# Queries and keys loaded in long runs, tokens in another order, in an attention and feed-forward kernel

## The chip, the cores and the metric

The kernel runs on one core of one Trainium2 chip. The metric is the device time of one execution in microseconds. TensorE is called PE below, VectorE DVE, ScalarE ACT, GpSimd POOL, and SyncE, which here only issues transfers, SP.

## What is computed

Attention with normalised queries and keys, for 8 batches, 12 heads, 448 tokens and 64 columns, and then a feed-forward block on the 3584 tokens (768 columns in, 1024 inside). All is float32; the feed-forward weights arrive as float64.

```python
q_n, k_n = rmsnorm(q, g_q), rmsnorm(k, g_k)          # over the 64 columns
scores = q_n @ k_n.T / sqrt(64)
attn = exp(scores - max); attn = attn / (sum(attn) + 1e-9)
x = (attn @ v) as (3584, 768)                        # heads side by side
h = x @ w_in                                         # (3584, 1024)
solu = h * softmax(h)
ln = (solu - mean) / sqrt(var + 1e-6) * g_ln
out = ln @ w_out                                     # (3584, 768)
```

The result doesn't depend on the order in which the keys are summed, and each token's row stands by itself from the attention to the output. So tokens may be held in any order inside, as long as the output rows are written to their places.

## The kernel before

The work has three stages that follow each other on PE: attention (to about 326 us), the first product of the feed-forward block (L982, to about 579 us) and the second (L1177, to the end). The two products are done in blocks that are added and subtracted first, so that seven products stand for eight; this has no part in the change.

**Attention.** Two heads of a batch make a pair (48 of them, `n`), and two pairs make a quad (24, `m`; its pairs are `a = 2m` and `b = 2m + 1`). A loop runs over the quads. The instructions of each engine are issued in the order in which the loop writes them, and each engine keeps its order. `unit(f)` runs a piece of PE work and then whatever was put off by `later`.

For each pair, except the first two, the loop calls these functions:

- `load(n)` (L627 to L637) reads q and k of the pair with eight transfers on SP's queue. A transfer takes 32 partitions. Partition `g * 32 + t` holds, for each of 14 blocks of 32 tokens, token `t` of that block: half a row, 32 columns (128 bytes). `g` stands for the head and the half of the columns. The tile `qk` has five buffers.
- `squares(n)` (L653) squares the tile on ACT, `row_sums(n)` (L660) sums each 32 columns on DVE, and `fold_sums(m)` (L668) adds the two halves of a row for a whole quad on POOL: four copies between partitions and a sum. `fold_one(n)` (L677) does it on DVE for one pair.
- `rsqrt_seed` (L690) makes the inverse root on ACT by Ln and Exp, and `rsqrt_step` (L697) improves it on DVE by a Newton step of four instructions.
- `normalise(n)` (L706) multiplies the tile by it on POOL, one instruction of 128 x 896.
- `qk_transpose(n)` (L720) transposes blocks of 32 x 32 on DVE, which gives `qkT` with the columns on the partitions and the tokens along them, and `gain(n)` (L725) multiplies the q half by the gains on ACT.
- `scores(n, kc)` (L804) makes three tiles of 128 keys, `scores_last(m)` (L818) the last 64 keys of both pairs. ACT takes the exponentials (L802). `values_last` and `values` (L846, L859) multiply by v, and `sums(m)` (L870) makes the row sums on PE from the last tile, E 2 and `es`, which `add(n)` (L836) prepares on DVE as E 0 + E 1.
- `inverse` and `divide` (L889, L905) divide by the sums, and `store_x(m)` (L914) writes the result to `xd` in the chip's memory.

The first two pairs are read by rows (`load_rows`, L732, in four transfers each on SP and ACT) and transposed on PE; `take_rows` (L780) copies them to `qkT`.

`load_v(m)` (L639) reads v for a quad with three transfers: 384 keys with three neighbouring keys on a partition, and the last 64 keys (`vl`) by head. Accordingly the keys of score tile `kc` are every third one (L811).

**The order in a quad.** From quad 4 on (`early`), the loop begins with `norms_next()`, the norms of the next quad's pairs. Then come `load_v` for the next quad, scores, `store_x` of the last quad, the transposes of the next quad's pairs, each followed by a load six pairs ahead, `add(a)`, then the squares, row sums, gains and fold for the pairs after the next, `add(b)`, the values and the sums. Quads 0 to 3 have an order of their own. There the norms stand later, and up to quad 4 (`scarce`) `squares(b + 4)` and its row sum stand behind the gains, around `add(b)`. In quad 0 pairs 2 and 3 are folded singly on DVE.

**The last stage.** Four tiles of 128 tokens make a period of 49 slots. In each the loop writes seven products of seven blocks, evacuates PE's banks with ACT (L1189) and DVE (L1191, L1209, L1221, L1229), and prepares the operands of the next period: `load_u` (L1111) reads a block (`ur`, eight per period) on SP, and `make` (L1127) turns it into an operand on ACT (L1132 to L1136) or DVE (L1138 to L1144). `store_y` (L1241) writes two tiles of 128 tokens by 384 columns with one transfer on SP, four per period, 28 in all. The re-reading of the weights (`again`, L585) goes through the same queue.

Of the kernel before, what the change touches and what calls it, by code (L numbers as in the profile page):

```python
# [14 lines left out]
OP = AluOpType  # L15
# [351 lines left out]
def fast_path(  # L367
# [259 lines left out]
    def load(n):  # L627
        b, hp = divmod(n, NP)
        h0 = 2 * hp
        d = st[n] = {}  # L630
        d["qk"] = loads.tile([P, 2, NB, 32], FP32, tag="qk", name="qk", bufs=5)
        for s, src in enumerate((q, k)):
            for g in range(4):
                nc.sync.dma_start(
                    d["qk"][g * 32 : g * 32 + 32, s],
                    src[b, h0 + g // 2].rearrange("(b t) (x d) -> x t b d", t=32, x=2)[g % 2],
                )  # L637

    def load_v(m, queue=nc.sync):  # L639


        d = quads[m] = {}
        b, hp = divmod(2 * m, NP)
        src = v[b, 2 * hp : 2 * hp + 4]
        d["v"] = loads.tile([P, 4, NJ, D], FP32, tag="v", name="v", bufs=2)
        d["vl"] = loads.tile([P, 2, D], FP32, tag="vl", name="vl", bufs=2)
        queue.dma_start(
            d["v"].rearrange("p h j d -> p h (j d)"), src[:, 0 : NJ * P].rearrange("h (p j) d -> p h (j d)", j=NJ)
        )
        for i in range(2):  # L650
            nc.sync.dma_start(d["vl"][i * D : (i + 1) * D], src[2 * i : 2 * i + 2, NJ * P : S].rearrange("h p d -> p h d"))

    def squares(n):  # L653
        d = st[n]
        d["sq"] = work.tile([P, 2 * NB, 32], FP32, tag="sq", name="sq", bufs=2)
        nc.scalar.activation(d["sq"], d["qk"].rearrange("p s b d -> p (s b) d"), AF.Square)  # L656
# [49 lines left out]
    def normalise(n, e=nc.gpsimd):  # L706
        d = st[n]
        if ("one", n) in norms:
            y = norms["one", n]["y"]
        else:  # L710
            y = norms[n // 2]["y"][:, n % 2 * 2 * NB : (n % 2 + 1) * 2 * NB]
        d["qkn"] = work.tile([P, 2 * NB, 32], FP32, tag="qkn", name="qkn", bufs=2)
        e.tensor_tensor(  # L713
            d["qkn"],
            d["qk"].rearrange("p s b d -> p (s b) d"),
            y.rearrange("p b -> p b ()").to_broadcast([P, 2 * NB, 32]),
            OP.mult,
        )
# [61 lines left out]
    def take_rows(n, s):  # L780
        d = st[n]
        if s == 0:
            d["qkT"] = work.tile([P, 2, S], FP32, tag="qkT", name="qkT", bufs=3)
            nc.scalar.activation(d["qkT"][:, 0], d["pt", 0], AF.Copy, scale=gcol[:, KF : KF + 1])
        elif n == 0:
            nc.scalar.copy(d["qkT"][:, 1], d["pt", 1])
        else:
            nc.vector.tensor_copy(d["qkT"][:, 1], d["pt", 1])


# [13 lines left out]
    def scores(n, kc):  # L804
        d = st[n]
        s = ps_t.tile([P, 2, 512], FP32, tag="t", name="s")

        for c in range(0, P, D):
            for h in range(2):
                hh = slice(h * D, (h + 1) * D)  # L810
                keys = slice(NJ * c + kc, NJ * (c + D - 1) + kc + 1, NJ)  # L811
                nc.tensor.matmul(  # L812
                    s[c : c + D, h, 0:S], d["qkT"][hh, 1, keys], d["qkT"][hh, 0, :],
                    start=True, stop=True,
                )
        exponentials(d, kc, s)
# [424 lines left out]
    def store_y(n, x, k, i):  # L1241
        r = (4 * n + 2 * k) * P
        nc.sync.dma_start(
            out[r : r + 2 * P, i * HO : (i + 1) * HO].rearrange("(t p) n -> p t n", p=P), x
        )
# [75 lines left out]
    with tc.manual_schedule():  # L1321
# [18 lines left out]
        rsqrt_step(st[1])  # L1340
        for m in range(NQ):
# [5 lines left out]


# [3 lines left out]
            if m == 0:  # L1352
                unit(lambda: scores(a, 0))
                normalise_rows(1, 0)
                normalise_rows(1, 1)
                unit(lambda: scores(a, 1))
                unit(lambda: scores(a, 2))
                for s in range(2):
                    transpose_rows(1, s)
                    take_rows(1, s)  # L1360
                squares(2)
                add(a)
                row_sums(2)
                fold_one(2)
                unit(lambda: scores_last(m))
                squares(3)
                rsqrt_seed(norms["one", 2])
                rsqrt_step(norms["one", 2])
                normalise(2)
                unit(lambda: scores(b, 0))  # L1370
                row_sums(3)
                fold_one(3)
                unit(lambda: scores(b, 1))
                unit(lambda: scores(b, 2))
                rsqrt_seed(norms["one", 3])
                rsqrt_step(norms["one", 3])
                normalise(3)
                qk_transpose(2)
                gain(2)
                add(b)  # L1380
                load_v(1)
                load(6)
                load(7)
                unit(outputs)
                squares(4)
                qk_transpose(3)
                gain(3)
                unit(lambda: values(b))
                squares(5)
                unit(lambda: sums(m))  # L1390
                inverse(m)
                row_sums(4)
                row_sums(5)
                fold_sums(2)
                later(1, lambda m=m: divide(m))
                continue
            early = 3 < m and next1
            def norms_next():
                rsqrt_seed(norms[m + 1])
                rsqrt_step(norms[m + 1])  # L1400
                normalise(a + 2)
                normalise(b + 2)

# [12 lines left out]
            if m == 3:  # L1416
                norms_next()
            unit(lambda: scores(a, 1))
            if m == 2:
                norms_next()  # L1420
            if 1 < m < 4:
                add(a)
            unit(lambda: scores(a, 2))
            if m == 3:
# [5 lines left out]
            if m < 2:  # L1430
                add(a)
            unit(lambda: scores(b, 0))
            if m == 1:
                norms_next()
                load(a + 6)
                load(b + 6)
            if m == 2:
                qk_transpose(a + 2)
                load(a + 6)
            unit(lambda: scores(b, 1))  # L1440
            if early or 1 < m < 4:
# [3 lines left out]
            if m > 3:  # L1445
                add(a)
            unit(lambda: scores(b, 2))
            if m == 1:
                qk_transpose(a + 2)
            scarce = m < 5  # L1450
            if next2:
                squares(a + 4)
                if not scarce:
                    squares(b + 4)
# [3 lines left out]
            if m == 1:  # L1458
                add(b)
                qk_transpose(b + 2)  # L1460
                squares(b + 4)
            if next1:
                gain(b + 2)
            if scarce and m > 1:
                squares(b + 4)
                add(b)
# [3 lines left out]
            if not scarce:  # L1470
                add(b)
# [214 lines left out]
```

## Time and profile before

| | us |
|---|---|
| median of 3 runs | 825.22 (821.91 to 825.55) |
| the profiled execution | 818.75 |
| its span, from the first instruction to the last | 816.9 |
| granted clock | 0.997 of full speed |
| PE busy | 799.7 (98% of the span) |
| DVE, POOL, ACT busy | 671.2, 464.0, 460.5 |
| transfer engines' busy share, 100 to 300 us | 0.68 to 0.83 |

How to read it: an engine's busy time is the time in which it had an instruction in work. SP's queue is shown by its issues; the length of an issue is what SP takes to hand a transfer over, not the transfer itself, whose landing is given apart. The page puts 86% of the chain that ended last on PE. PE's own waits are short, and all of them are in the first 84 us and from 540 us on:

| PE waits | us |
|---|---|
| second product, for ACT's copy u (L1189) | 3.2 |
| sums, for es (L839) | 1.4 |
| last scores, for E (L802) | 1.3 |
| second product, for POOL's sums (L1156) | 1.0 |
| scores, for E (L802) | 0.9 |
| first scores, for qkT (L786) | 0.8 |

Transfers on SP's queue that the change touches:

| | issues | KB each | us to landing |
|---|---|---|---|
| qk, from q and from k | 184 and 184 | 56.0 | 2.3 and 2.1 |
| v | 24 | 384.0 | 4.6 |
| vl | 48 | 32.0 | 4.0 |
| output | 28 | 384.0 | 3.6 and 2.6 |

### The profile page before, as it was taken

How to read it: one execution, taken by the hardware profiler on the slowest of the kernel's cores; microseconds unless marked ns; L12 is line 12 of the kernel's file. 1: busy time of each engine (PE TensorE's matmuls, PEld its weight loads, DVE VectorE, ACT ScalarE, POOL GpSimd, SP SyncE). 2: the span in 40 equal slices, each digit the busy share in tenths (PEclk: the TensorE clock that was granted, in tenths of full speed). 3: DMA queues.
4: the chain of work that ended last, by engine and by line, in shares of the span. 5: the costliest groups of instructions: out<-in, count | busy, mean ns of one | idle time of the engine just before them, and what ended most of it. 6: DMA issues, size and time to landing. Idle time of an engine off the chain costs nothing.

```text
span 816.9 us, 14941 instructions
## 1 busy us (share of the span) xinstructions
PE 799.7 (98%) x5030; PEld 470.3 (58%) x5030; DVE 671.2 (82%) x1203; ACT 460.5 (56%) x757; POOL 464.0 (57%) x635
## 2 busy tenths in 40 slices
PE   8999999999999999999999999999899999999996
PEld 4333444444444443444444444444689999999996
DVE  6867888897887978589999999998996776866944
ACT  6676778786786865355655444432425455464410
POOL 1334546556554567222254378776487867777861
PEclk9999999999999999999999999999999999999999
DMA  7777778787778744335555435543448457466312
GB/s 138 145 144 190 165 173 201 152 205 148 170 165 170 161 97 123 100 91 153 155 150 147 116 90 149 143 124 79 146 149 273 134 188 250 126 227 219 110 59 83
DMA packets 271938, 122.74 MB, mean 150 GB/s; under 512 B 190444, under 2 KB 257004, under 8 KB 271852
## 3 DMA queue, kind: packets, MB, share of 16 engines
q1 hardware_dynamic: 256668, 111.79, 52.2%
q10 hardware_dynamic: 15184, 9.90, 4.3%
q8 instruction: 42, 0.69, 0.3%
q14 instruction: 44, 0.36, 0.1%
HBM read 84.94 MB, written 36.70 MB: 149 GB/s over the span
## 4 chain that ended last, share of the span: by engine, by line
PE 86%; DVE 3%; POOL 2%; issue 1%; ACT 0%; DVEq 0%; POOLq 0%
PE b L982 31%; PE A L1177 14%; PE o L865 11%; PE s L812 11%; PE B L1177 7%; PE sm L884 5%; PE C L1177 3%; PE s L825 2%; PE o L854 2%; POOL sums L1156 0%; POOL sums L1155 0%; POOL sums L1158 0%; DVE bs L1054 0%; DVE ub L1075 0%; DVE part L664 0%
## 5 line engine op out<-in xcount | busy, mean ns | idle before, releaser
L982 PE MATMUL b<-w_in,xg 128*128 128x512 f32 x336 | 151.1, 592 | 0.0
L802 ACT ACTIVATE E<-s 128x896 f32<-128x896 f32 x168 | 139.1, 935 | 17.1 <-PE s L812 16.8
L812 PE MATMUL s<-qkT 64*64 64x448 f32 x1152 | 120.7, 546 | 1.7 <-ACT E L802 0.9
L982 PE MATMUL b<-w_in,xsum 128*128 128x512 f32 x252 | 115.0, 592 | 0.0
L865 PE MATMUL o<-E,v 128*64 128x448 f32 x576 | 113.5, 543 | 0.0
L982 PEld LDWEIGHTS b<-w_in,xg 128*128 128x128 f32 x336 | 63.8, 190 | 80.2 <-issue 76.4
L713 POOL TENSOR_TENSOR qkn<-qk,ny 128x896 f32<-128x896 f32 x46 | 78.6, 1729 | 26.9 <-DMA qk<-in_k_dram 12.2
L674 POOL COPY ss<-part 32x56 f32<-32x56 f32 x88 | 42.2, 479 | 88.7 <-DVE part L664 86.0
L1177 PE MATMUL A<-w_out,sums 128*128 128x192 f32 x392 | 80.7, 329 | 4.0 <-ACT u L1189 2.6
L812 PEld LDWEIGHTS s<-qkT 64*64 64x64 f32 x1152 | 48.1, 163 | 60.1 <-ACT E L802 30.0
L982 PEld LDWEIGHTS b<-w_in,xsum 128*128 128x128 f32 x252 | 47.9, 190 | 60.3 <-issue 57.6
L1060 POOL TENSOR_TENSOR he<-he,mhalf 128x1 f32<-128x1 f32 x28 | 17.1, 610 | 114.3 <-DVE he L1059 112.2
L865 PEld LDWEIGHTS o<-E,v 128*64 128x64 f32 x576 | 39.2, 137 | 72.7 <-issue 68.5
L1177 PE MATMUL B<-w_out,sums 128*128 128x192 f32 x392 | 79.8, 326 | 0.0
L1066 ACT ACTIVATE u<-u,shift,he 128x1024 f32<-128x1024 f32 x28 | 34.7, 1239 | 74.7 <-POOL shift L1062 72.0
L1177 PEld LDWEIGHTS A<-w_out,sums 128*128 128x128 f32 x392 | 66.7, 191 | 5.3 <-issue 2.9
L1177 PEld LDWEIGHTS B<-w_out,sums 128*128 128x128 f32 x392 | 66.3, 190 | 0.2
L723 DVE STREAM_TRANSPOSE qkT<-qkn 128x896 f32<-128x896 f32 x46 | 48.7, 1090 | 6.1 <-POOL qkn L713 6.1
L839 DVE TENSOR_TENSOR es<-E 128x896 f32<-128x896 f32 x48 | 53.2, 1111 | 0.5 <-ACT E L802 0.5
L563 POOL TENSOR_TENSOR w_out<-w_out 128x384 f32<-128x384 f32 x44 | 50.8, 1159 | 1.9
L664 DVE TENSOR_REDUCE part<-sq 128x28 f32<-128x896 f32 x46 | 48.1, 1076 | 2.1 <-ACT sq L656 0.2
L1177 PE MATMUL A<-w_out,s 128*128 128x192 f32 x224 | 46.1, 329 | 0.6 <-ACT u L1189 0.6
(143 smaller groups left out, 1497.3 us busy)
## 6 DMA issues: line engine op xcount, KB each, us to landing
ur<-ud SPq DMA_DIRECT2D x60, 256.0 KB, 4.5
ud<-ub SPq DMA_DIRECT2D x112, 128.0 KB, 2.2
xd<-xo SPq DMA_DIRECT2D x24, 448.0 KB, 3.3
qk<-in_q_dram SPq DMA_DIRECT2D x184, 56.0 KB, 2.3
qk<-in_k_dram SPq DMA_DIRECT2D x184, 56.0 KB, 2.1
v<-in_v_dram SPq DMA_DIRECT2D x24, 384.0 KB, 4.6
out_dram<-P SPq DMA_DIRECT2D x21, 384.0 KB, 3.6
raw<-in_moe_w_in_dram SPq DMA_DIRECT2D x12, 512.0 KB, 4.9
```

What stands on the lines that cost most here:

```text
L563: nc.gpsimd.tensor_tensor(o, p, q, OP.subtract)
L664: nc.vector.tensor_reduce(norms[m]["part"][:, i], st[n]["sq"], AX, OP.add)
L674: e.tensor_copy(ss[g * 32 : g * 32 + 32], part[o * 32 : o * 32 + 32])
L713: e.tensor_tensor(d["qkn"], d["qk"].rearrange("p s b d -> p (s b) d"), y.rearrange("p b -> p b ()").to_broadcast([P, 2 * NB, 32]), OP.mult,)
L723: nc.vector.transpose(d["qkT"].rearrange("p s t -> p (s t)"), d["qkn"].rearrange("p b d -> p (b d)"))
L802: nc.scalar.activation(d["E", kc], s[:, :, 0:S], AF.Exp)
L812: nc.tensor.matmul(s[c : c + D, h, 0:S], d["qkT"][hh, 1, keys], d["qkT"][hh, 0, :], start=True, stop=True,)
L839: nc.vector.tensor_tensor(d["es"], d["E", 0], d["E", 1], OP.add)
L865: nc.tensor.matmul(d["o"][h * D : (h + 1) * D, :], quads[n // 2]["v"][:, n % 2 * 2 + h, kc], d["E", kc][:, h], start=False, stop=(kc == NJ ...
L884: nc.tensor.matmul(sm[g : g + 32, :], ones[:, w], e[:, h, t * S // 2 : (t + 1) * S // 2], start=(x == 0), stop=(x == len(terms) - 1),)
L982: nc.tensor.matmul(o, a[:, c], w_in[i][:, c], start=(c == 0), stop=(c == HD - 1))
L1177: nc.tensor.matmul(k[bank], a[:, c].rearrange("p a i -> p (a i)"), w_out[:, area, i, c], start=begin and c == 0, stop=c == KC - 1, skip_gr ...
```

## The change

Token `t * 14 + b` takes the place of token `b * 32 + t`. So partition `t` of a head holds 14 neighbouring tokens, which lie together in memory: 14 x 64 values. A transfer of `load` takes one run of 14 x 64 - 32 values (3456 bytes) per partition, once from the first column on and once from column 32 on, so that the wanted half of each token begins each 64 values of the tile. The other half is loaded with it and not used; the tile is twice as wide, and has four buffers instead of five. The transfers stay eight per pair.

`own(n)` names the wanted halves. `normalise` writes q with one instruction and k with two, which also puts the blocks of keys in the order in which a score tile's 128 keys lie side by side; `take_rows` does the same for the first two pairs, with one more instruction for k. `load_v` reads v in the same order of keys, with eight transfers of 32 partitions instead of three. `store_y` writes 32 rows at a time, since 32 neighbouring partitions now hold tokens that lie 14 rows apart: eight transfers instead of one.

The order in the first quads changes too. In quad 0 `squares(2)` comes before the first scores, pairs 2 and 3 are folded together on POOL and share their norms' chain, and the loads of pairs 6 and 7 come earlier. Quads 2 and 3 get the order that held from quad 4 on, quad 1 nearly so, and the special places of `squares(b + 4)` and `add(b)` up to quad 4 are gone.

```diff
 def load(n):
-        d["qk"] = loads.tile([P, 2, NB, 32], FP32, tag="qk", name="qk", bufs=5)
+        d["qk"] = loads.tile([P, 2, NB, D], FP32, tag="qk", name="qk", bufs=4)
         for s, src in enumerate((q, k)):
             for g in range(4):
+                x = g % 2 * 32
                 nc.sync.dma_start(
-                    d["qk"][g * 32 : g * 32 + 32, s],
-                    src[b, h0 + g // 2].rearrange("(b t) (x d) -> x t b d", t=32, x=2)[g % 2],
+                    d["qk"][g * 32 : g * 32 + 32, s].rearrange("p b d -> p (b d)")[:, 0 : NB * D - 32],
+                    src[b, h0 + g // 2].rearrange("(t b) d -> t (b d)", t=32)[:, x : x + NB * D - 32],
                 )
+    def own(n):
+        return st[n]["qk"][:, :, :, 0:32]
 def load_v(m, queue=nc.sync):
-        src = v[b, 2 * hp : 2 * hp + 4]
+        src = v[b, 2 * hp : 2 * hp + 4].rearrange("h (t b) d -> t h b d", t=32)
-        queue.dma_start(
-            d["v"].rearrange("p h j d -> p h (j d)"), src[:, 0 : NJ * P].rearrange("h (p j) d -> p h (j d)", j=NJ)
-        )
-        for i in range(2):
-            nc.sync.dma_start(d["vl"][i * D : (i + 1) * D], src[2 * i : 2 * i + 2, NJ * P : S].rearrange("h p d -> p h d"))
+        for g in range(4):
+            queue.dma_start(
+                d["v"][g * 32 : g * 32 + 32].rearrange("p h j d -> p h (j d)"),
+                src[:, :, NJ * g : NJ * g + NJ].rearrange("t h j d -> t h (j d)"),
+            )
+        for g in range(4):
+            i = g // 2 * 2
+            queue.dma_start(d["vl"][g * 32 : g * 32 + 32], src[:, i : i + 2, NJ * 4 + g % 2])
 def normalise(n, e=nc.gpsimd):
-        e.tensor_tensor(
-            d["qkn"],
-            d["qk"].rearrange("p s b d -> p (s b) d"),
-            y.rearrange("p b -> p b ()").to_broadcast([P, 2 * NB, 32]),
-            OP.mult,
-        )
+        x, z = own(n), d["qkn"].rearrange("p (s b) d -> p s b d", s=2)
+        y = y.rearrange("p (s b) -> p s b", s=2)
+        for s, (i, j) in ((0, (0, NB)), (1, (0, 4 * NJ)), (1, (4 * NJ, NB))):
+            o, c, f = z[:, s, i:j], x[:, s, i:j], y[:, s, i:j]
+            if s == 1 and i == 0:
+                o = o.rearrange("p (j g) d -> p g j d", g=4)
+                c = c.rearrange("p (g j) d -> p g j d", g=4)
+                f = f.rearrange("p (g j) -> p g j ()", g=4).to_broadcast([P, 4, NJ, 32])
+            else:
+                f = f.rearrange("p b -> p b ()").to_broadcast([P, j - i, 32])
+            e.tensor_tensor(o, c, f, OP.mult)
 def scores(n, kc):
-                keys = slice(NJ * c + kc, NJ * (c + D - 1) + kc + 1, NJ)
+                keys = slice(P * kc + c, P * kc + c + D)
 def store_y(n, x, k, i):
-        r = (4 * n + 2 * k) * P
-        nc.sync.dma_start(
-            out[r : r + 2 * P, i * HO : (i + 1) * HO].rearrange("(t p) n -> p t n", p=P), x
-        )
+        rows = out[:, i * HO : (i + 1) * HO].rearrange("(a t b) n -> a t b n", t=32, b=NB)
+        for t in range(2):
+            c = (4 * n + 2 * k + t) * 4
+            for g in range(4):
+                a, b = divmod(c + g, NB)
+                nc.sync.dma_start(rows[a, :, b], x[g * 32 : g * 32 + 32, t])
 # the loop, quad 0
+        squares(2)                                   # ahead of the first scores
             unit(lambda: scores(a, 1))
-            unit(lambda: scores(a, 2))
+            row_sums(2)
             (transpose_rows(1, s), take_rows(1, s) for both s)
-            squares(2); add(a); row_sums(2); fold_one(2)
+            unit(lambda: scores(a, 2))
+            squares(3); row_sums(3); fold_sums(1); add(a)
             unit(lambda: scores_last(m))
-            squares(3); rsqrt_seed, rsqrt_step, normalise(2)
             unit(lambda: scores(b, 0))
-            row_sums(3); fold_one(3)
+            norms_next(); load_v(1); load(6); load(7)
             unit(lambda: scores(b, 1)); unit(lambda: scores(b, 2))
-            rsqrt_seed, rsqrt_step, normalise(3)
+            squares(4); row_sums(4)
             qk_transpose(2); gain(2)
+            squares(5)
             add(b)
-            load_v(1); load(6); load(7)
             unit(outputs)
# the loop, from quad 1 on
-            early = 3 < m and next1
+            early = 1 < m and next1
...
-            if 1 < m < 4:
-                add(a)
...
             if next2:
                 squares(a + 4)
-                if not scarce:
-                    squares(b + 4)
+                squares(b + 4)
                 row_sums(a + 4)
             if next1:
                 gain(a + 2)
                 gain(b + 2)
-            if scarce and m > 1:
-                squares(b + 4)
-                add(b)
             if next2:
                 row_sums(b + 4)
                 fold_sums(m + 2)
-            if not scarce:
-                add(b)
+            add(b)
```

## The prediction

> **What bounds the kernel now.** First the page's busy shares, then who TensorE (PE) waits for, then its timeline.
>
> ```profile
> PE 799.7 (98%) x5030; PEld 470.3 (58%) x5030; DVE 671.2 (82%) x1203; ACT 460.5 (56%) x757; POOL 464.0 (57%) x635
> ```
>
> PE is busy in all but 17 of 816.9 us. Its timeline (start, length, instruction) shows where the rest is:
>
> ```profile
> 10.24 2.52 PE L812 MATMUL s<-qkT 64*64 64x448 f32 x24 [0.79 <-ACT qkT L786]
> ...
> 25.75 2.52 PE L812 MATMUL s<-qkT 64*64 64x448 f32 x24
> ...
> 39.40 1.77 PE L812 MATMUL s<-qkT 64*64 64x448 f32 x16
> ...
> 54.19 1.77 PE L812 MATMUL s<-qkT 64*64 64x448 f32 x16
> ...
> 68.60 2.52 PE L812 MATMUL s<-qkT 64*64 64x448 f32 x24
> ...
> 82.89 1.39 PE L812 MATMUL s<-qkT 64*64 64x448 f32 x12
> ```
>
> These are the starts of quads 0 to 5. Later ones come every 12.90 us to the end of attention (95.78, then 108.68), without a wait. So quads 0 to 4 last 15.5, 13.7, 14.8, 14.4 and 14.3 us and lose 2.6, 0.8, 1.9, 1.5 and 1.4 us against that period: 8.2 us, the most that a better load stage can return. From 610 to 810 us PE is again full; any stall there counts whole. The end is a store on SP's queue:
>
> ```profile
> 801.60 0.38 SPq L1243 DMA_DIRECT2D out_dram<-P  x1
> ...
> 807.91 0.38 SPq L1243 DMA_DIRECT2D out_dram<-C  x1
> 809.40 1.73 SPq L1243 DMA_DIRECT2D out_dram<-P  x2
> ```
>
> The last issue starts at 810.76; the queue's wait for its landing ends at 814.6, and closing takes until 816.9. So the price of an issue on SP matters most:
>
> ```profile
> 372.85 1.80 SPq L515 DMA_DIRECT2D raw<-in_moe_w_out_dram  x4
> ...
> 5.78 2.04 SPq L634 DMA_DIRECT2D qk<-in_k_dram  x4
> 7.87 2.05 SPq L634 DMA_DIRECT2D qk<-in_q_dram  x4
> ```
>
> Four q/k issues of 448 short pieces take 2.09 us, 0.52 each; four issues of 32 rows in one piece (w_out, 3072 bytes) take 1.84 with the gap, 0.46 each. An issue costs nearly the same whatever it moves.
>
> **Loads.** 368 issues stay 368, each of 32 rows in one piece: 0.46 instead of 0.52 by the w_out row. Per quad 16 of them save 0.9 us on SP. v goes from one issue (0.47 with its gap) and two for vl (0.65 each) to eight. Four by 0.47 to 0.51 (v's row, and ud's, also 32 rows) and four by 0.46 to 0.65 (w_out's row, vl's row) make 3.7 to 4.6 instead of 1.8. With xd's 0.6 and 0.25 of waits SP needs 11.9 to 12.9 us per quad, before 11.0 and some late issues; I take 12.35. In twelve quads a w_in load adds 0.5, so SP has nothing to spare beside PE's 12.9. Load 7 was fully issued at 34.96; now it is 3.69, six q/k loads by 3.7, two v loads by 4.3 and grow's 0.75: 35.2. The loads do not come earlier.
>
> DMA time: the qk landing took 2.1 to 2.3 us with 128-byte pieces, w_out's 2.3 with 3072, so a load lands about as before. q/k bytes grow from 20.6 to 39.8 MB, some 66 GB/s more over 290 us, beside 150 to 200; the page has a slice of 273, so this is hidden. With four buffers, load a+6 waits for normalise(a+2), which at quad 2 ends near 44.5 where SP comes to it at 52: nothing.
>
> The Trainium skill, "DMA: Bandwidth & Descriptors", Specifications, has 512 bytes as the least transfer for line rate, which speaks for this change; by it alone the loads would land sooner and nearly all the 8.2 us would return, but these landings do not show it.
>
> **Early quads.** Quads 2 to 4 take the order that later quads have, with the norms at the head and add(b) after both row sums; that would return 1.9 + 1.5 + 1.4 = 4.8 us. Quad 1 pays: squares(7) now stands ahead of both gains and its row sum ahead of add(b). The load lands at 35.2 + 1.9 = 37.1; square 1.0, row sum 1.1 and add 1.1 end at about 40.3, while PE wants es 12 us into a quad begun near 26.2, at 38.2: +2.0. In quad 0 squares(2) stands ahead of the first exponential (its load, issued by 7.4, is there), the fold moves from DVE to POOL (four copies 1.0, sum 0.3) and the pair shares one chain; ACT's Ln waits for it with two exponentials behind, and the first take_rows is three reads instead of two on the path (L786's wait): about +0.4. Net -4.8 + 2.0 + 0.4 = -2.4. Bounds: -8.2, and +4 where SP needs its upper 12.9 plus w_in and PE has to follow.
>
> **Normalise on POOL.** One instruction becomes three.
>
> ```profile
> 97.80 3.36 POOL L713 TENSOR_TENSOR qkn<-qk,ny 128x896 f32<-128x896 f32 x2
> 105.72 2.58 POOL L674 COPY ss<-part 32x56 f32<-32x56 f32 x4 [4.56 <-DVE part L664]
> ```
>
> Smallest POOL instructions (rc copies, four in 0.89) put a further one at 0.2 to 0.25, so each normalise costs 1.68 + 0.45 = 2.1 us; 2.75 if priced as three separate products (w_out's 384 columns took 1.16: 1.35 + 1.16 + 0.25). The cover is thin. A ring repeats each quad: fold 2.97, Ln and Exp 0.65, Newton step 0.75, two normalises 3.36, the second transpose 1.05, add 1.1, row sums 2.2, gaps 0.27: 12.35 of 12.90 us in a quad with a weight join. 0.9 more makes 13.25, 0.35 too long; add(b) is 1.6 us ahead of PE, which hides four such quads, and a quad without a join recovers. Taken: +0.5 (0 to +10). Behind the late transpose on DVE queue add(a), row sums and add(b), which PE's sums want. The squares read 32 of 64 columns: nothing, below ACT's other work; key columns now side by side: 0 to -2 us on PE, taken 0, as three score groups of four take 2.26 to 2.34 us (0.75 to 0.78 each) and values' groups of two 4.66 / 6 = 0.78.
>
> **Stores.** 28 issues become 224. In the last stage SP issues a store in 8 by 0.46 = 3.7 instead of 0.43 us. Behind it queue the ur loads. The period from 640 us:
>
> ```profile
> 648.54 0.40 SPq L1243 DMA_DIRECT2D out_dram<-C  x1
> 648.99 0.96 SPq L1114 DMA_DIRECT2D ur<-ud  x2
> 650.62 0.39 SPq L1243 DMA_DIRECT2D out_dram<-P  x1
> 651.05 0.47 SPq L1114 DMA_DIRECT2D ur<-ud  x1
> ```
>
> The first ur now goes out at 652.3 and lands 2.8 to 4.5 later, 655.1 to 656.8; ACT's copy of it ran at 654.35. The later ones slip by 5.5 us: DVE's s1 at 660.25 gets its data at 661.3 or later. Behind both queue evacuations of PE's banks, which have some 1.4 us to spare (2.6 between two products of a bank, less 0.8 and 0.35). So 0 to 2.3 us per period, six periods: 0 to 14; nearer the low landing, since issues are now spread: 0.3 each, +2.
>
> At the end 24 issues follow 807.91: the last begins at 807.91 + 23 x 0.463 = 818.6 and lands 2.2 later (ud, 128 KB), 820.8 instead of 814.6: +6.2. With the shortest issue seen (0.31 and its gap, 0.354) +3.7, with q/k's 0.52 +7.5. The Trainium skill, same page, "Issuing engines are not separate DMA queues", calls the sequencer's time to start a DMA usually small beside the DMA; by it the tail would not grow and the sum would be 0.1. The tail's rows say the opposite.
>
> **Sum:** -2.4 + 0.5 + 2.0 + 6.2 = +6.3 us. The profiled execution took 818.75 (span 816.9), so 825 there; the runs shown have a median of 825.22, so 831.5. About 0.5% (4.1 us) is what a measurement of this kernel tells from no change.
>
> **The rivals.**
> - *Issue-bound middle* (slower, +10 to +16): ur lateness costs PE 1 to 2 us in each of six periods, or three-part normalises cost 2.75 and the POOL ring sets the period (0.5 us in some 15 quads). For: both slacks are about 1 us. Against: landings when issues are spread are the short ones, and POOL's small instructions are cheap. +6.3 + 7 = 838.5.
> - *Cheap issues* (faster): place SP's queue; an issue of 32 single pieces costs 0.354 in a row of them too. Load 7 then is out at about 28 and quads 0 to 4 all run in 12.9: -8.2, tail +3.7, no stall: -4.5, 820.7. It decides from about 0.38 per issue downward. For: the first of each w_out group takes 0.31. Against: the followers take 0.42.
> - *It cancels*: the issue is as forecast or a little less, but early quads return 5 to 6 and ur hides fully: 0 to +2, 826.
>
> **How the numbers follow.** Forecast 0.50 (own range 827.5 to 835), issue-bound 0.20, cancels 0.18, cheap issues 0.12. Slower by over 0.5%: 0.38 of the forecast and 0.20, 0.58; faster 0.10; the rest 0.32. The range 820 to 840 holds most of all four cases, and leaves out the ends of both outer ones.
>
> **What would show it.** Right: qk issues near 0.42 us; the last store issue at about 818; eight issues per store with ur behind them; quads 2 to 4 near 12.9 and quad 1 near 15. Wrong: store issues of 0.31 in a row, a quad period other than 12.9, PE waits on L1177 that grow past 2 us a period, or early quads that keep their 14 us.

## The result, and the profile after

The changed kernel takes 863.81 us (863.27 to 865.03) against 825.19: ratio 1.0479, 95% interval 1.0450 to 1.0508. The forecast was 831.5 with 840 as its upper end. The profiled executions took 863.27 and 818.75, their spans are 861.5 and 816.9. The stages, from the records of the two traces (first matmul of a product, DVE's read of a flag that follows the last result by 0.2 to 0.5 us, end):

| stage, us | before | after | forecast of the difference | difference |
|---|---|---|---|---|
| attention | 326.5 | 345.2 | -1.9 | +18.7 |
| first product | 252.5 | 252.5 | 0 | 0 |
| second product | 232.2 | 248.9 | +2.0 | +16.7 |
| tail behind it | 5.7 | 14.9 | +6.2 | +9.2 |

The page after, its busy shares and then the chain that ended last, by engine:

```profile
PE 810.7 (94%) x5030; PEld 460.8 (53%) x5030; DVE 665.6 (77%) x1190; ACT 461.4 (54%) x756; POOL 474.9 (55%) x732
...
PE 54%; SPq 17%; DMA 11%; DVE 6%; POOL 5%; issue 4%; ACT 3%; ACTq 0%; DVEq 0%; POOLq 0%
```

PE idles 50.8 us instead of 17.2, and is itself busy 11 us longer (the last section says how much of that is explained). The chain now runs through SP's queue: 17% of the span, where PE alone had carried 86% of it.

**Attention.** PE's timeline, the first scores of quads 6, 7 and 8:

```profile
98.81 2.49 PE L832 MATMUL s<-qkT 64*64 64x448 f32 x24
...
112.69 2.49 PE L832 MATMUL s<-qkT 64*64 64x448 f32 x24
...
126.54 2.49 PE L832 MATMUL s<-qkT 64*64 64x448 f32 x24
```

A quad takes 13.9 us, not 12.90. Here is SP's queue over one quad, from one weight load to the next (start, length of the group, line):

```profile
120.24 0.42 SPq L510 DMA_DIRECT2D raw<-in_moe_w_in_dram  x1
120.76 1.80 SPq L653 DMA_DIRECT2D v<-in_v_dram  x4
122.61 2.24 SPq L659 DMA_DIRECT2D vl<-in_v_dram  x4
124.99 0.38 SPq L936 DMA_DIRECT2D xd<-xo  x1
125.48 1.92 SPq L635 DMA_DIRECT2D qk<-in_q_dram  x4
127.44 1.81 SPq L635 DMA_DIRECT2D qk<-in_k_dram  x4
129.36 1.76 SPq L635 DMA_DIRECT2D qk<-in_q_dram  x4
131.16 2.92 SPq L635 DMA_DIRECT2D qk<-in_k_dram  x4
134.13 0.42 SPq L510 DMA_DIRECT2D raw<-in_moe_w_in_dram  x1
```

It hardly rests: 13.89 us for 26 issues, and PE follows. Four issues of one shape take 1.81 with the gaps between them, 0.463 from start to start. Two groups are longer. In the last one, 2.92, one issue took 1.53 us. In the vl group, 2.24, the fourth issue waited; the queue's waits from 100 to 300 us name it:

```profile
SPq L659 <- DMA raw<-in_moe_w_in_dram: 10.1, 10, 1.6
```

The trace shows eight semaphores that all DMAs take in turn, and each issue waits until its semaphore's last DMA has landed. The fourth vl issue stands 8 places behind the weight load (512 KB, landing in 4.9 us).

**Second product.** Who PE waits for from 598 to 847 us (total, times, longest):

```profile
PE A L1197 <- DVE u L1211: 12.4, 6, 3.2
```

The same wait before:

```profile
PE A L1177 <- DVE u L1191: 0.4, 1, 0.4
```

So 12.0 of the 16.7 us are this wait; PE's busy time in the stage grew by the other 4.7 (from 226.8 to 231.5). SP's queue in one of the periods shows rows of eight store issues with the loads of ur between them:

```profile
662.93 3.59 SPq L1270 DMA_DIRECT2D out_dram<-P  x8
...
669.36 3.56 SPq L1270 DMA_DIRECT2D out_dram<-C  x8
672.96 0.90 SPq L1134 DMA_DIRECT2D ur<-ud  x2
673.96 4.89 SPq L1270 DMA_DIRECT2D out_dram<-P  x8
678.90 0.42 SPq L1134 DMA_DIRECT2D ur<-ud  x1
...
681.31 4.92 SPq L1270 DMA_DIRECT2D out_dram<-P  x8
686.32 0.85 SPq L1134 DMA_DIRECT2D ur<-ud  x2
```

The last ur goes out at 686.8, 23.9 us behind the period's first store issue at 662.93. The same two groups before:

```profile
642.12 0.39 SPq L1243 DMA_DIRECT2D out_dram<-P  x1
...
655.64 1.62 SPq L1114 DMA_DIRECT2D ur<-ud  x2
```

The second ur of that last group started at 656.94, 14.8 us behind the store.

**Tail.** The last 24 store issues:

```profile
843.53 4.82 SPq L1270 DMA_DIRECT2D out_dram<-C  x8
848.45 8.56 SPq L1270 DMA_DIRECT2D out_dram<-P  x16
```

### The profile page after: what moved, and what is told of

The parts are those of the page before. It is cut to its first block, busy times and chain, and to the rows that moved or that the text cites. A ratio compares the mean times of both kernels' runs of the same rounds, so it can differ in the third digit from the quotient of the medians.

```text
span 861.5 us, 15450 instructions
## 1 busy us (share of the span) xinstructions
PE 810.7 (94%) x5030; PEld 460.8 (53%) x5030; DVE 665.6 (77%) x1190; ACT 461.4 (54%) x756; POOL 474.9 (55%) x732
## 4 chain that ended last, share of the span: by engine, by line
PE 54%; SPq 17%; DMA 11%; DVE 6%; POOL 5%; issue 4%; ACT 3%; ACTq 0%; DVEq 0%; POOLq 0%
PE b L1002 29%; SPq L635 13%; PE A L1197 10%; PE B L1197 5%; DMA ur<-ud 3%; PE o L885 3%; DMA raw<-in_moe_w_in_dram 3%; PE s L832 2%; PE C L1197 2%; DMA qk<-in_k_dram 2%; POOL ss L682 2%; DVE part L672 2%; SPq L1270 1%; ACT sq L664 1%; SPq L653 1%
## 5 line engine op out<-in xcount | busy, mean ns | idle before, releaser
L832 PE MATMUL s<-qkT 64*64 64x448 f32 x1152 | 123.0, 555 | 2.4 <-ACT E L822 1.4
L682 POOL COPY ss<-part 32x56 f32<-32x56 f32 x92 | 46.6, 506 | 119.8 <-DVE part L672 116.9
L1197 PE MATMUL A<-w_out,sums 128*128 128x192 f32 x392 | 82.9, 335 | 16.2 <-DVE u L1211 12.4
L731 POOL TENSOR_TENSOR qkn<-qk,ny 128x448 f32<-128x448 f32 x138 | 90.3, 689 | 13.0 <-POOL rc L923 4.3
L832 PEld LDWEIGHTS s<-qkT 64*64 64x64 f32 x1152 | 37.8, 133 | 71.7 <-ACT E L822 37.9
L664 ACT ACTIVATE sq<-qk 128x896 f32<-128x896 f32 x46 | 44.3, 971 | 31.6 <-DMA v<-in_v_dram 14.5
L736 DVE STREAM_TRANSPOSE qkT<-qkn 128x896 f32<-128x896 f32 x46 | 50.9, 1106 | 12.7 <-POOL qkn L731 12.7
```

The costliest lines, as they stand in the source:

```text
L664: nc.scalar.activation(d["sq"].rearrange("p (s b) d -> p s b d", s=2), own(n), AF.Square)
L682: e.tensor_copy(ss[g * 32 : g * 32 + 32], part[o * 32 : o * 32 + 32])
L731: e.tensor_tensor(o, c, f, OP.mult)
L736: nc.vector.transpose(d["qkT"].rearrange("p s t -> p (s t)"), d["qkn"].rearrange("p b d -> p (b d)"))
L832: nc.tensor.matmul(s[c : c + D, h, 0:S], d["qkT"][hh, 1, keys], d["qkT"][hh, 0, :], start=True, stop=True,)
L1197: nc.tensor.matmul(k[bank], a[:, c].rearrange("p a i -> p (a i)"), w_out[:, area, i, c], start=begin and c == 0, stop=c == KC - 1, skip_gr ...
```

## The experiments

All were run beside the kernel before, whose medians were 822.7 to 824.4. "First five" below is the sum of quads 0 to 4 (before 72.6 us, after 75.3), "quad" the mean of quads 8 to 21 (12.90 and 13.84). The kernel after and experiments 1, 11 and 14 have the same attention, instruction by instruction, and it ended at 345.2, 351.5, 349.3 and 346.2: about 6 us of its length are chance. The second product of the seven runs that keep the stores in rows of eight and the last stage of the kernel after (after and experiments 2, 3, 4, 8, 10 and 13) took 244.7 to 252.3.

The theories: A, the number of DMA issues on SP's queue is the whole loss; B, the doubled bytes of q and k and their landing; C, four buffers instead of five; D, the eight DMAs that can be in flight; E and F for the order and the number of the store pieces.

**1. Stores whole again, in the kernel after**

```diff
-        for t in range(2):
-            ...
-            for g in range(4):
-                nc.sync.dma_start(rows[a, :, b], x[g * 32 : g * 32 + 32, t])
+        r = (4 * n + 2 * k) * P
+        nc.sync.dma_start(out[r : r + 2 * P, ...].rearrange("(t p) n -> p t n", p=P), x)
```

> The kernel after, with each half of a result tile stored by one DMA of 128 rows again (28 store issues instead of 224); the rows of the output stay in the order of the chunks, which is not the reference's. Theory A (issues on SP's queue): the stores alone made the second product 16.9 us and the tail 9.0 us longer, so both go: second product from 248.1 to 231-234 us, tail from 15.5 to 6.5-8, time 838-841, attention unchanged at 345 us. Theory B (the doubled q and k bytes and their landing): stores have no part in it, at most the tail shrinks: 855-864.

Measured: 841.00 us, ratio 1.0194 (1.0163 to 1.0225). Second product 232.2, tail 5.3; attention 351.5. The split stores are the whole loss of both stages, 16.7 and 9.6 us.

**2. v in three loads, in the kernel after**

```diff
-        for g in range(4):
-            queue.dma_start(d["v"][g * 32 : g * 32 + 32]..., src[:, :, NJ * g : NJ * g + NJ]...)
-        for g in range(4):
-            queue.dma_start(d["vl"][g * 32 : g * 32 + 32], ...)
+        queue.dma_start(d["v"]..., src[:, 0 : NJ * P].rearrange("h (p j) d -> p h (j d)", j=NJ))
+        for i in range(2):
+            nc.sync.dma_start(d["vl"][i * D : (i + 1) * D], ...)
```

> The kernel after, with v of a quad loaded by 3 DMAs in the old order of keys instead of 8 (same bytes; the values are then paired with other keys than the scores, so the output is not the reference's). Theory A (issues): SP has 5 issues of 0.47 us less to do in each quad, 2.35 us, so that its 13.0-13.3 us fall under the 12.9 us of PE: quads of 12.9-13.0, attention's end from 345.3 to 327-331, time 845-850. Theory B (bytes and landing): the bytes are the same, quads stay at 13.7, time 860-864. Theory C (four q/k buffers instead of five, SP waits for GpSimd's normalise): the waits stay, but SP catches up behind them: 848-858.

Measured: 845.88, ratio 1.0271 (1.0243 to 1.0298); attention ends at 328.7, second product and tail stay (248.1, 15.0). PE's timeline has the old period back:

```profile
97.99 2.49 PE L829 MATMUL s<-qkT 64*64 64x448 f32 x24
...
110.85 2.49 PE L829 MATMUL s<-qkT 64*64 64x448 f32 x24
...
123.72 2.49 PE L829 MATMUL s<-qkT 64*64 64x448 f32 x24
```

12.86 and 12.87 us. Five issues fewer per quad, with the same bytes, are the 16.5 us (16.5 to 22.8 against the four runs of one attention named above).

**3. Five buffers for q and k, in the kernel after**

```diff
-        d["qk"] = loads.tile([P, 2, NB, D], FP32, tag="qk", name="qk", bufs=4)
+        d["qk"] = loads.tile([P, 2, NB, D], FP32, tag="qk", name="qk", bufs=5)
```

> The kernel after, with five buffers for q and k instead of four, and nothing else. Theory A (issues alone): SP's 13.1 us of issues per quad remain, quads go from 13.7 to 13.1 at the least if its gaps of some 0.9 us were only a matter of order: 850-860. Theory B (bytes and landing): no change, 862-865. Theory C (the fourth buffer makes SP wait for the normalise): SP's gaps go and the quads fall to 12.9-13.1: time 847-851.

Measured: 863.88, ratio 1.0477; attention 345.9, quad 13.86. The fourth buffer is not the bound.

**4. Single loads of 128-byte pieces in the new order of tokens**

```diff
-                    d["qk"][...][:, 0 : NB * D - 32],
-                    src[b, h0 + g // 2].rearrange("(t b) d -> t (b d)", t=32)[:, x : x + NB * D - 32],
+                    d["qk"][g * 32 : g * 32 + 32, s],
+                    src[b, h0 + g // 2].rearrange("(t b) (x d) -> x t b d", t=32, x=2)[g % 2],
```

> The kernel after, with q and k loaded once, in runs of 32 values (128 bytes) as before, in the new order of tokens, into five buffers as before; v in 8 issues and the stores by 32 rows stay. Theory A (issues): an issue of 0.521 us again instead of 0.463, 16 of them, 0.9 us more of SP in each quad: quads of 13.7-14.5, time 863-878. Theory B (bytes and landing): half the bytes of q and k and a landing of 2.1-2.3 us again: quads 12.9-13.1, time 845-850. Theory C (buffers): as in the kernel with five buffers and full loads, 847-860.

Measured: 929.68, ratio 1.1292; attention 410.4, quad 16.67. Half the bytes and one buffer more, and 66 us slower than after. An issue of q or k took 0.620 us here (0.477 before, with as many pieces of the same size but in another order of rows), 0.665 from start to start. The first product is untouched at 252.5. The issue's price sets the quad; theory A, the nearest, had taken 0.521 for the price.

**5. Experiments 1 and 2 together**

The diff is the sum of both.

> The kernel after, with v of a quad by 3 DMAs in the old order of keys and each half of a result tile stored by one DMA: the two edits that gave 18 us and 20 us alone, together. Values are paired with other keys and output rows stay in chunk order, so the output is not the reference's. What stays of the change: the doubled q and k loads, the order of tokens in scores and transposes, three products for a normalise, the loop's new order. Theory A (numbers of issues are the whole loss): attention 328.7, first product 252.5, second 232.2, tail 5.3, sum 818.7 us of span against 816.9 of the kernel before: time 824-829. Theory B (the doubled bytes or the loop's order cost on their own once the issues are gone): 832-840.

Measured: 820.45, ratio 0.9969 (0.9947 to 0.9991). Attention 326.6, second product 232.9, tail 5.4; the time is below the 824 to 829 of theory A. With the numbers of issues undone nothing of the loss is left, though the doubled bytes, the order of tokens, the three-part normalise and the new loop are all in. Quads 2 to 4 took 13.0, 13.6 and 12.9.

**6. The new loop alone, in the kernel before.** The loop over quads is copied from the kernel after (its diff is in the change above).

> The kernel before, with the loop over quads of the kernel after and nothing else of the change (loads, keys, stores and the single product of a normalise as before). Its first five quads took 72.7 us before, 75.4 after. Theory of the forecast (the new order starts the norms of a quad sooner): first five quads 68-71 us, time 819-823. Rival (the new order itself makes quads 0 and 1 late, 0.8 and 3.5 us, and returns 2.4 in quads 2 to 4): 74-75 us, time 825-828.

Measured: 824.42, ratio 1.0028 (1.0007 to 1.0049); first five 73.8 (16.1, 16.6, 14.6, 13.6, 12.9), attention 330.8, because three later quads took 13.7 to 14.3. The rival is the nearer: quads 0 and 1 pay more than quads 2 to 4 return.

**7 and 8. v issued from ScalarE, one load after each unit of work; in the kernel before and in the kernel after**

```diff
-        queue.dma_start(
+        issue(
...
+                later.append(lambda: nc.scalar.dma_start(o, x))
...
     def unit(f, steps=4):
         ...
         f()
+        if vq:
+            vq.pop(0)()
```

> The kernel before, with the 3 loads of v of a quad issued one by one from ScalarE between its units of work instead of from SP. If SP's queue makes the first quads late (72.7 us for five that would be 64.5 at 12.9): SP is relieved of 1.7 us a quad and the first five quads take 67-71 us, time 818-822. Rival (ScalarE is as scarce, its issues of about 0.4 us stand ahead of the exponentials): PE waits on E grow, time 825-832.

> The kernel after, with the 8 loads of v of a quad issued one by one from ScalarE between its units of work instead of from SP; output as the reference's. Theory A (SP's queue is the bound of attention): SP has 3.8 us less in each quad, quads of 12.9 to 13.1 from quad 4 on, attention's end 329-333 instead of 345.3, time 847-852. Theory D (not SP but the number of DMAs counts, 8 semaphores shared in turn by all queues, an issue waiting until the one 8 places before has landed): quads stay at 13.4-13.9, time 856-864. Rival (ScalarE's 3.8 us more a quad make its exponentials late): PE waits on E grow to 10-20 us, time 852-862.

Measured: 853.74, ratio 1.0364, and 873.94, ratio 1.0616; quad 14.29 and 14.18. Both are slower than without it, more than any theory had. SP's waits from 80 to 320 us in the second one:

```profile
SPq L635 <- DMA v<-in_v_dram: 49.2, 40, 3.9
SPq L635 <- DMA raw<-in_moe_w_in_dram: 16.0, 10, 2.1
```

q and k need nothing of v. SP waits for a semaphore that an earlier DMA in program order holds, and ScalarE issues that DMA late, behind its exponentials. The shared semaphores tie the two queues together, so the experiments do not tell what SP gains when it is relieved. PE's own waits on E, which the rival had put at 10 to 20 us, were 5.8 us in all from 80 to 320 us in the second one.

**9. Both splits in the kernel before**

```diff
+        for g in range(4):
+            queue.dma_start(d["v"][g * 32 : g * 32 + 32]..., src[:, 32 * NJ * g : 32 * NJ * (g + 1)]...)
+        for g in range(4):
+            ...
+            nc.sync.dma_start(d["vl"][g * 32 : g * 32 + 32], ...)
...
+        for t in range(2):
+            for g in range(4):
+                j = r + t * P + g * 32
+                nc.sync.dma_start(out[j : j + 32, ...], x[g * 32 : g * 32 + 32, t])
```

> The kernel before, in its own order of tokens and with the right output, with v of a quad loaded by 8 DMAs of 32 partitions and each half of a result tile stored by 8 DMAs of 32 rows; q, k, the loop and the normalise as before. Theory A (numbers of issues are the whole loss): the second product 248-250 us instead of 232.2 and the tail 14.5-15 instead of 5.7, as in the kernel after; in attention an issue of q or k still has a pitch of 0.521 us, not 0.463, so 16 of them with 8 of v at 0.47, xd and a weight load need 14.0-15.0 us of SP a quad: attention's end 350-366 instead of 326.5, worse than after's 345.3; time 867-884. Theory B (the doubled bytes of q and k had a part in the loss): attention 330-340, time 855-863.

Measured: 885.41, ratio 1.0774; attention 366.2, second product 249.4, tail 14.9, quad 14.81. The two splits alone, without anything else of the change, cost 63 us, just above theory A's numbers and far from B's.

**10. Weight loads issued from GpSimd, in the kernel after**

```diff
-            nc.sync.dma_start(to, w[c * P : (c + 1) * P])
+            nc.gpsimd.dma_start(to, w[c * P : (c + 1) * P])
```

> The kernel after, with the loads of w_in that run beside attention (512 KB each, 4.9 us to land) issued from GpSimd instead of SP, and nothing else. An issue on SP waits until the DMA 8 places before it has landed; the last issue of v stands 8 places behind such a load and waited 1.0-2.0 us for it, 12 times, 13.3 us in all. Theory D (these waits are a part of the loss): both go, the wait and the issue of 0.47 us, 1.1-1.5 us in each quad that has such a load: quads of 12.9-13.3 where they took 13.8-15.1, attention's end 331-337 instead of 345.3, time 850-856. Theory A alone (issue time only): 0.47 us in each of 12 quads, attention 339-341, time 857-860. Rival (an issue on GpSimd costs its ring more than SP gains): 862-870.

Measured: 867.38, ratio 1.0570; attention 350.5, quad 13.96. Inconclusive: the wait of vl on the weight load went, but the load itself then took 7.0 us to land, and v's issues waited 13.6 us in 17 places for earlier q loads. The waits moved and the sum stayed.

**11. The pieces of a store one in each slot of the second product, in the kernel after**

```diff
-                nc.sync.dma_start(rows[a, :, b], x[g * 32 : g * 32 + 32, t])
+                pieces.append((rows[a, :, b], x[g * 32 : g * 32 + 32, t]))
...
             for f in at.pop(slot, ()):
                 f()
+            if pieces:
+                nc.sync.dma_start(*pieces.pop(0))
```

> The kernel after, with the 8 pieces of a store handed to SP one in each slot of the second product, not 8 in a row, so that loads of ur and of the second weight read come in between; the same number of issues. Theory E (the second product lost its 16.9 us because ur queues behind rows of 8 store issues, 3.7 us each): ur is issued near its own time, DVE's waits on ur and on the result tiles fall from 25 us to 5-10, the second product takes 234-240 us instead of 248.9, time 849-856; the tail stays near 15. Rival F (the number of issues itself, or the result tiles that come free later still): 246-254 us, time 861-867.

Measured: 849.04, ratio 1.0319 (1.0279 to 1.0359). Second product 231.9 with all 224 issues, tail 15.0, attention 349.3. SP's queue in the same period:

```profile
671.62 0.42 SPq L1134 DMA_DIRECT2D ur<-ud  x1
672.09 0.43 SPq L1625 DMA_DIRECT2D out_dram<-C  x1
672.56 0.42 SPq L1134 DMA_DIRECT2D ur<-ud  x1
673.03 1.37 SPq L1625 DMA_DIRECT2D out_dram<-C  x3
674.44 0.42 SPq L1134 DMA_DIRECT2D ur<-ud  x1
```

ur goes out between the pieces, and PE's waits on DVE's u are back at what they were before:

```profile
PE A L1197 <- DVE u L1211: 0.4, 1, 0.4
```

In this stage it was the order on the queue, not the number.

**12. The new order from quad 2 on, in the kernel before**

```diff
-            early = 3 < m and next1
+            early = 1 < m and next1
...
-            scarce = m < 5
+            scarce = m < 2
```

(and the special places of quads 2 and 3 taken out)

> The kernel before, with the loop's new order from quad 2 on only (norms of the next quad at the head of a quad), quads 0 and 1 in the old order; loads, keys and stores as before, output as the reference's. The whole new order gave quads 0 and 1 3.6 us more and quads 2 to 4 2.4 us less. Theory (the two are independent): first five quads 70-71 us instead of 72.7, time 820-823. Rival (what quads 2 to 4 win is only what SP caught up with during the long quad 1): first five quads 72-74, time 823-826.

Measured: 824.33, ratio 1.0022 (0.9998 to 1.0047); first five 72.6, as before: 15.5, 13.7, 14.8, 13.8, 14.9. The rival holds: alone, the order returns nothing there. Attention ended at 331.1, as six later quads took 13.2 to 14.0; whether that is the order or chance was not tested.

**13. Half the bytes of q and k, with every issue kept, in the kernel after**

```diff
-                    ...rearrange("(t b) d -> t (b d)", t=32)[:, x : x + NB * D - 32],
+                    ...rearrange("(t b) d -> t (b d)", t=32)[:, x : x + NB * 32],
```

> The kernel after, with each load of q and k cut to the first 448 values of a run (1792 bytes instead of 3456); the blocks are read from those, so the heads hold wrong values and the output is not the reference's, but every instruction and every issue stays. Theory A (SP's issue time is the price): the pitch of an issue stays 0.463, quads stay at 13.7-14.1, attention's end 343-351, time 860-868. Theory D (eight in flight at most, so the landing sets the pace): landing falls from 2.9 to 2.0-2.4 us, the waits of issues on earlier landings go, quads of 12.9-13.2, attention 327-334, time 844-851.

Measured: 858.78, ratio 1.0415 (1.0373 to 1.0457); attention 341.6, quad 13.80. The DMA issues of the kernel after and of this run (number, KB each, median us to landing):

```profile
qk<-in_q_dram SPq DMA_DIRECT2D x184, 108.0 KB, 2.9
...
qk<-in_q_dram SPq DMA_DIRECT2D x184, 56.0 KB, 1.9
```

Landing fell from 2.9 to 1.9 and the quad did not follow: the pitch of an issue is still 0.463, and the quad goes with it. Attention is 4 to 10 us shorter than in the four runs named above; against the kernel after nearly all of it lies in quads 4 to 8. That may be chance or a small share of the bytes.

**14. Experiment 11, and the last pieces from two queues**

```diff
+                q = nc.scalar if slot > end - 8 and len(pieces) % 2 else nc.sync
+                q.dma_start(*pieces.pop(0))
...
+        for i, x in enumerate(pieces):
+            (nc.sync, nc.scalar)[i % 2].dma_start(*x)
```

> The kernel after with the store pieces spread over the slots, and the pieces that are left when the second product ends issued alternately from SP and from ScalarE, which has nothing to do there; output as the reference's. Theory A (the tail is the number of issues left on one queue, about 22 of 0.463 us behind the last result): the tail falls from 15.0 to 9-11 us, time 843-846 where the spread stores alone took 849. Rival (the landings and the eight in flight set it): the tail stays at 13-15, 847-850.

Measured: 845.60, ratio 1.0267 (1.0233 to 1.0300); tail 12.4 instead of 15.0, second product 232.8. Half of what theory A put on it: three of the last issues took 1.91 to 2.14 us each, two on SP and one on ScalarE. It is the fastest version of the new order with all its loads and stores, and still slower than before. The only one with a ratio below 1, experiment 5, pairs values with other keys and stores its rows in another order.

## Why the prediction was wrong, step by step

**The price of an issue was right.** Its w_out row gave 0.46; q and k came to 0.463, v to 0.474, v's eight to 3.8 us (3.7 to 4.6 forecast). The rival of cheap issues is out.

**The step that failed in attention is "SP needs 11.9 to 12.9 us per quad", of which the prediction took 12.35.** Added up from start to start, in a quad with a weight load: 16 x 0.463 + 8 x 0.473 + 0.43 for xd + 0.47 = 12.1. Two terms were missing. One issue in each quad is long: 17 of them between 90 and 320 us took 0.86 to 1.81 us, some 1.0 more than the others. The trace before has such issues too (30 of 335 took over 0.7 us in the same stretch); the prediction spoke of "some late issues" there and had no such term in its sum. Of waits it had 0.25, and 0.3 came, but the wait on the weight load's landing added another 0.6. SP's time in quads 8 to 21, added up from the issues in the traces, in us per quad:

| run | issues | at their usual pitch | long ones beyond it | waits | quad |
|---|---|---|---|---|---|
| v in three | 19.7 | 9.6 | 0.5 | 2.7 | 12.86 |
| after | 25.7 | 12.0 | 1.0 | 0.9 | 13.84 |
| before, split | 25.7 | 12.9 | 1.0 | 0.9 | 14.81 |
| narrow, new order | 25.7 | 15.2 | 0.7 | 0.8 | 16.67 |

In the first row 2.1 of the waits are for DVE's result xo: SP is ahead there, and PE's period is the floor. In the other rows 0.5 to 0.6 of them are for the weight load. Because the sum lay near 12.9, the 1.6 us that were left out decided all: they went from "nothing to spare" to 0.9 us in each of 18 quads, 16 us, where the prediction allowed +4 at most.

**Early quads.** Forecast -2.4, measured +2.7. Quads 0 and 1 paid 1.0 and 3.6 (0.4 and 2.0 forecast), quads 2 to 4 returned 1.8 instead of 4.8. The new loop alone, in the kernel before (experiment 6), paid 0.6 and 3.0 and returned 2.4. What was wrong is the reason: without the longer quads 0 and 1 the order returns nothing (experiment 12). Behind a long quad 1 and with fewer issues, experiments 2 and 5 returned 2.5 and 4.1 with the same attention, instruction by instruction; how much of that is room on SP and how much chance was not told apart.

**Normalise on POOL.** Right that POOL has the room, as experiment 5 loses nothing by it; two cost 0.57 us more, 3.93 instead of 3.36, where the prediction had 0.9. **Doubled bytes.** Right that they are hidden (experiments 5 and 13), wrong on the landing, which grew to 2.9 and 3.0.

The Trainium skill, "DMA: Bandwidth & Descriptors", Specifications, sets 512 bytes as the least piece for line rate. Two runs with the same 56 KB per load agree in direction: 1.9 us in pieces of 1792 bytes (experiment 13), 2.5 in pieces of 128 (experiment 4). It did not help, as the landing was not what attention waited for. Its section "Issuing engines are not separate DMA queues" calls the time to start a DMA usually small beside the DMA; for one DMA that holds here, 0.463 against landings of 1.6 to 3.6. In sum it does not: landings overlap and issues on one queue do not, so 25.7 issues per quad, or the 24 at the end, take longer than any landing.

**Stores: 0.3 us per period, +2.0, is the step that failed in the second product.** Measured 16.7, 2.8 per period. The prediction saw that ur queues behind the stores and moved the first ur by 3.7 and the later by 5.5 us; the last one came 9 us later. It then took the short end of its own range (0 to 14) on the ground that issues are now spread, while they stand in rows of eight; in the period shown one issue took 1.5 us and the last row waited 1.8 us for earlier landings. The rival of an issue-bound middle had this mechanism, with 1 to 2 us per period; its other half, POOL's ring, did not happen.

**Tail.** The mechanism was right, 24 issues in a row at the end, only the size was off: 9.2 instead of 6.2. 23 x 0.463 is 10.65 us; from 843.53 the last issue started at 856.59, 13.06 later, as two of them took 1.67 and 1.65 us.

Of the signs that the prediction named, those of its mechanisms came (q and k issues of 0.42 us, eight issues to a store with ur behind them), and so did three of those against its sizes: another period of the quads, first quads that keep their 14 us, and waits of PE on the second product past 2 us a period.

## What to carry to other kernels

Add up a DMA queue as one adds up an engine: every issue from start to start, whatever its size, plus the long issues and the waits on earlier landings that the trace already shows, and compare the sum with the period of the engine that bounds the stage; where the two lie as near as here (12.35 to 12.85 forecast against 12.9), a term left out decides. When a store must be split, hand its pieces out one by one between the loads that others wait for; in a row they delay all of them, and at the end of the program each one counts whole. A layout that makes one DMA cheaper to issue (0.463 instead of 0.521 us) can still lose if it multiplies the DMAs elsewhere.

## What the runs showed of the hardware that was not expected

**A stall can cost PE twice.** In the kernel after, PE waited 2.40 us before the last sums of a quad; the timeline and the windows behind it (PE busy, PEld, DVE, ACT, POOL, then the granted clock):

```profile
43.65 0.58 PE L904 MATMUL sm<-es,ones 128*32 128x224 f32 x8 [2.40 <-DVE es L859]
44.16 4.18 PE L832 MATMUL s<-qkT 64*64 64x448 f32 x24
```

```profile
44.00:48.00 4.00, 4.00 (x32) 1.50 (x28) 3.11 (x9) 2.25 (x4) 3.09 (x9) 0.57 0.91 239
48.00:52.00 4.00, 4.00 (x44) 1.37 (x36) 3.44 (x5) 3.76 (x6) 2.32 (x5) 1.00 0.80 231
```

The granted clock was 0.57 for four microseconds, and 24 matmuls took 4.18 us instead of 2.49: 1.7 us more on top of the 2.4. The kernel after has four such stretches of 3.4 us at a granted clock of 0.50 (from 44.4, 604.2, 686.2 and 757.8 us on) while PE works, the kernel before one (from 586.6). Three more at 1.7 us are 5 of PE's 11 us of added busy time; its 5030 matmuls are the same, and where the other 6 come from was not found. Nor does every stall bring it, as the wait of another period shows, and the window behind it with a granted clock of 1.00:

```profile
793.47 0.73 PE L1197 MATMUL A<-w_out,sums 128*128 128x192 f32 x3 [2.48 <-DVE u L1211]
```

```profile
793.40:797.40 4.00, 3.93 (x24) 3.96 (x25) 3.48 (x9) 0.21 (x1) 2.23 (x3) 1.00 0.82 256
```

The Trainium skill, "TensorE: Matmul & The Clock Gate", Part 1, has the clock halve after an idle window of about 3.4 us; here a wait of 2.40 was followed by it, and one of 2.48 was not.

**The price of an issue depends on the order of the rows in memory**, not on the number of pieces alone: 0.477 and 0.620 us for two loads of 448 pieces of 128 bytes each. **One issue in some 25 on SP is long**, 0.7 to 2 us, in attention and in the tail alike: 17 of 426 between 90 and 320 us of the kernel after, 15 of 353 in experiment 4, 12 and 15 of 335 in experiments 2 and 5, two of the last 24. The kernel before has more, 30 of 335. What causes it was not found. **Queues are tied by eight shared semaphores:** a DMA moved to another engine that issues it late holds up the queue that it came from (49.2 us in 40 waits of SP in experiment 8).
